# Attention chunks taken from four sequences in turn, scores masked by VectorE on their way out of PSUM, and first-expert weight loads tied to later blocks

## The chip, the core and the metric

The kernel runs on one core of a Trainium2 chip. The metric is the device time of one execution in microseconds (us). TensorE (PE) multiplies matrices, VectorE (DVE), ScalarE (ACT) and GpSimd (POOL) work on elements, and SyncE (SP) issues the transfers. Each engine takes its own instructions strictly in the order in which they stand.

## What is computed

Three layers stand one after another. The tokens are 4 sequences of 768; a head has 48 columns, there are 8 heads, and 384 columns in all.

```python
# layer 1: decayed linear attention, per sequence and head
for t in range(S):
    state = alpha[:, :, t, :, None] * state + np.einsum('bhd,bhe->bhde', k[:, :, t], v[:, :, t])
    y[:, :, t] = np.einsum('bhd,bhde->bhe', q[:, :, t], state)
# layer 2: SiLU feed-forward, 384 -> 2048 -> 384
h = x @ w_in
x = (h * (1.0 / (1.0 + np.exp(-h)))) @ w_out
# layer 3: one expert of eight for each token, 384 -> 1024 -> 384, times its gate
expert_idx = np.argmax(logits, axis=1)
out[mask] = gate_w[mask, None] * (np.maximum(x[mask] @ w1[e], 0.0) @ w2[e])
```

## The kernel before

**Tiles.** Attention works on chunks of 128 tokens. There are 24, six to a sequence (`CPB` = 6), and chunk n belongs to sequence n // 6. The feed-forward works on 8 blocks of 384 tokens, so that three chunks make a block; a block takes 16 steps f. Each step is `mm1` (9 products, then SiLU on ACT, a second ACT copy and a DVE subtraction that split the result into a high and a low fp16 half) and `mm2` (9 products). Every operand of a product is split into a high and a low half; three products stand for one in full precision. At the end of a block `route` picks the expert of each token and scatters the token's row into a list of that expert (the first DVE instruction of `route` is `lg`, L868, three to a block). The experts then run over 29 tiles of 128 rows.

**One attention chunk.** `att_A` makes running products of the decays (DVE scans). `att_Bk` and `att_Bq` scale keys and queries. `att_C` multiplies them into two score tiles in PSUM, which ACT copies out with a scale (L676) and GpSimd masks in place by `affine_select` (L677). `att_S` splits each masked tile: ACT copies the high half (L687), DVE subtracts to get the low half (L688). `att_KT` scales the keys on GpSimd (L696), splits them (L698, L699) and turns them by a transposing DMA. `att_D` adds score and state products into `yp` (L716 with the state, L723 with the scores); `att_move` sends the result by a transposing DMA into the block's input. `att_U` multiplies keys and values (`up`, L752), decays the state on GpSimd (L759), adds on DVE (L764, or L768 in the first chunk of a sequence) and splits the state for the next chunk (`st`: ACT L770, DVE L771). A chunk that is the first of its sequence has no state to read; one that is the last has no `att_KT` and no `att_U`. Two state tiles take turns.

**Weights.** `conv_w` turns the feed-forward weights from float64 words into fp16 halves; this runs in the first block. `load_w1` loads one 512 KB piece of an expert's first matrix into the staging tile `work` and splits it (L492 on ACT, L493 on DVE); 16 such pieces, rows 0 to 255 of eight experts, make `weights_a`, and later generators hold the rest. `pump_w` starts one piece.

**What sets the order.** `block` writes the steps out, with `pump_j` taking one attention step before and after each `mm1`, and `pump_w` one weight piece every fourth f from block 1 on. The framework's scheduler then puts the instructions of each engine in an order of its own, and issues early what nothing holds back. `after` adds a dependency only to hold an instruction back: here the first two pieces of `weights_a` wait for `gates[8]`, the `mm1` of step 8 in block 0; the other pieces wait only for their half of `work`.

Of the kernel before, what the change touches and what calls it, by code (L numbers as in the profile page):

```python
# [272 lines left out]
def attention_silu_moe_kernel(  # L273
# [78 lines left out]
    nc.gpsimd.iota(tok, pattern=[[128, NCH]], base=0, channel_multiplier=1)  # L352
# [19 lines left out]
    if True:  # L372
# [61 lines left out]
        state = [stat.tile([128, NPAIR, 2 * D], FP32, name=f"state{i}") for i in range(2)]  # L434
# [122 lines left out]
        def load_w1(c, e):  # L557
            st = work[:, F * (e % 2):F * (e % 2 + 1)]
            ins = nc.sync.dma_start(out=st, in_=w1[e, c * 128:(c + 1) * 128, :])
            if c == 0 and e < 2:  # L560
                after(ins, gates[KF // 2])
            split(st, SW1, w1s["h"][c][:, e, :], w1s["l"][c][:, e, :])
            if c == 0:
                nc.vector.tensor_reduce(
                    out=guard("w1", 2.0 ** -6), in_=st[:, 0:64], axis=AXX, op=ALU.max, apply_absolute_value=True
                )
# [19 lines left out]
        def att_load(n, names):  # L586
            if n >= NCH:
                return
            b, c = divmod(n, CPB)
            for nm in names:  # L590
                t = nat[nm][n % len(nat[nm])]
                nc.sync.dma_start(
                    out=t[:, :, 0:D], in_=att_src[nm][b, :, c * 128:(c + 1) * 128, :].rearrange("h p d -> p h d")
                )
                ch.setdefault(n, {})[nm] = t
# [57 lines left out]
        def att_Bq(n):  # L653
            d = ch[n]
            pq = transpose4(flat(d["q"]))
            Q = a2.tile([128, NPAIR, 128], FP32, tag="Q", name="Q", bufs=1)
            nc.vector.scalar_tensor_tensor(out=Q, in0=d["P"], scalar=PCLIP, in1=pq, op0=ALU.min, op1=ALU.mult)
            d["Q"] = Q
            if n % CPB:
                qs = d["qs"] = a2.tile([128, 2, NPAIR, 128], FP16, tag="qs", name="qs", bufs=1)  # L660
                nc.scalar.activation(out=qs[:, 0], in_=Q, func=ACTF.Copy)
                nc.gpsimd.tensor_sub(out=qs[:, 1], in0=Q, in1=qs[:, 0])

        def att_C(n):
# [9 lines left out]
            for i in range(2):  # L674
                s = a2.tile([128, NPAIR, 128], FP32, tag="S", name="S")
                nc.scalar.activation(out=s, in_=sc[i], func=ACTF.Copy, scale=SST)  # L676
                nc.gpsimd.affine_select(  # L677
                    out=s, in_=s, pattern=[[0, NPAIR], [1, 128]], compare_op=ALU.is_ge, fill=0.0, base=0,
                    channel_multiplier=-1,
                )  # L680
                d["S"].append(s)

        def att_S(n):
            d = ch[n]
            ss = d["ss"] = a2.tile([128, 2, 2, NPAIR, 128], FP16, tag="ss", name="ss", bufs=1)
            for i, s in enumerate(d.pop("S")):
                nc.scalar.activation(out=ss[:, i, 0], in_=s, func=ACTF.Copy)  # L687
                nc.vector.tensor_sub(out=ss[:, i, 1], in0=s, in1=ss[:, i, 0])  # L688

        def att_KT(n):  # L690
            d = ch[n]
            if n % CPB == CPB - 1:
                return
# [12 lines left out]
        def att_D(n, g):  # L706
            d = ch[n]
            c = n % CPB
# [34 lines left out]
        def att_U(n):  # L743
            d = ch.pop(n)
            c = n % CPB
# [10 lines left out]
            new, old = state[(c + 1) % 2], state[c % 2]  # L756
            if c:
                wide = d["pe"][:, 1].rearrange("r (p o) -> r p o", o=1).to_broadcast([128, NPAIR, 2 * D])
                nc.gpsimd.tensor_tensor(out=new, in0=old, in1=wide, op=ALU.mult)  # L759
# [9 lines left out]
            st = ch[n + 1]["st"] = a2.tile([128, 2, NPAIR, 2 * D], FP16, tag="st", name="st")  # L769
            nc.scalar.activation(out=st[:, 0], in_=new, func=ACTF.Copy)  # L770
            nc.vector.tensor_sub(out=st[:, 1], in0=new, in1=st[:, 0])  # L771
# [44 lines left out]
        def mm1(j, f):  # L816
# [9 lines left out]
            if j == 0:  # L826
                gates[f] = ins
            g, gh, gl = g_u[f % 3]
# [381 lines left out]
        def block(j):  # L1210
# [8 lines left out]
            for f in range(KF):  # L1219
# [10 lines left out]
                if j and (f % 4 == 1 or done[0] >= NCH):  # L1230
                    pump_w()
# [118 lines left out]
```

## Time and profile before

| | us |
|---|---|
| median of 3 runs | 847.2 (845.36 to 847.26) |
| profiled execution | 848.5 |
| its span | 846.9 |
| PE busy in the span | 758.5 |
| DVE busy | 517.5 |
| ACT busy | 441.0 |
| POOL busy | 256.6 |

Busy time is an average over stages which have different limits, so the span is read in stretches. On PE a row's duration includes the filling of the pipeline, so that a PE that shows as busy need not be at its peak. The chain of waits of the page covers only the last instructions and is of no use here.

### The profile page before, as it was taken

How to read it: one execution, taken by the hardware profiler on the slowest of the kernel's cores; microseconds unless marked ns; L12 is line 12 of the kernel's file. 1: busy time of each engine (PE TensorE's matmuls, PEld its weight loads, DVE VectorE, ACT ScalarE, POOL GpSimd, SP SyncE). 2: the span in 40 equal slices, each digit the busy share in tenths (PEclk: the TensorE clock that was granted, in tenths of full speed). 3: DMA queues.
4: the chain of work that ended last, by engine and by line, in shares of the span. 5: the costliest groups of instructions: out<-in, count | busy, mean ns of one | idle time of the engine just before them, and what ended most of it. 6: DMA issues, size and time to landing. Idle time of an engine off the chain costs nothing. (4 is left out here: it accounts for less than half of the span.)

```text
span 846.9 us, 16786 instructions
## 1 busy us (share of the span) xinstructions
PE 758.5 (90%) x5544; PEld 466.8 (55%) x5544; DVE 517.5 (61%) x1480; ACT 441.0 (52%) x953; POOL 256.6 (30%) x332
## 2 busy tenths in 40 slices
PE   5246899899999999999899999999688999999996
PEld 4144666556667666666657655555344554555553
DVE  8889899797787786766656486475552222222221
ACT  4456567776566565556555575666532222222221
POOL 4465221245453444234335112121331111111011
PEclk8556999999999999999999999999999999999999
DMA  9983754875445534413601146254767657655662
GB/s 203 266 237 60 162 135 129 202 182 112 94 77 107 89 70 87 80 46 72 82 27 36 32 150 178 75 141 147 173 160 143 127 112 105 110 119 106 115 122 63
DMA packets 250363, 100.23 MB, mean 118 GB/s; under 512 B 231305, under 2 KB 239662, under 8 KB 250144
## 3 DMA queue, kind: packets, MB, share of 16 engines
q1 hardware_dynamic: 246880, 89.50, 50.2%
q0 software_dynamic: 3392, 9.57, 3.3%
q8 instruction: 51, 0.84, 0.4%
q14 instruction: 40, 0.33, 0.1%
HBM read 58.40 MB, written 12.36 MB: 84 GB/s over the span
## 5 line engine op out<-in xcount | busy, mean ns | idle before, releaser
L843 PE MATMUL o<-wo_h,w2l 128*128 128x392 f16 x528 | 146.2, 330 | 9.1 <-ACT w2l L830 3.6
L822 PE MATMUL hp<-w2h,wi_h 128*128 128x384 f16 x576 | 145.9, 330 | 5.3 <-DMA w2h<-ys 3.0
L1140 DVE SCALAR_TENSOR_TENSOR work<-hp,work 128x512 f16<-128x512 f32 x58 | 40.0, 690 | 118.7 <-ACT work L1139 118.6
L1133 PE MATMUL hp<-w1h,xT 128*128 x348 | 106.1, 387 | 3.5 <-DVE work L1140 2.9
L843 PEld LDWEIGHTS <-w2l 128*128 128x128 f16 x792 | 73.8, 98 | 62.1 <-ACT w2l L830 5.8
L822 PEld LDWEIGHTS <-wi_h 128*128 128x128 f16 x768 | 74.1, 98 | 52.1 <-issue 8.2
L822 PE MATMUL hp<-w2h,wi_l 128*128 128x384 f16 x288 | 95.0, 330 | 1.3 <-DVE wi_l L493 1.3
L1133 PEld LDWEIGHTS <-xT 128*128 128x128 f16 x522 | 51.7, 99 | 64.6 <-issue 8.7
L843 PE MATMUL o<-wo_l,w2l 128*128 128x392 f16 x264 | 86.9, 329 | 0.0
L1168 POOL DMA_INDIRECT out_dram<-ob,mt x29 | 28.2, 972 | 188.5 <-ACT ob L1165 182.1
L1139 ACT ACTIVATE work<-hp 128x512 f16<-128x512 f32 x58 | 34.6, 596 | 72.5 <-PE hp L1133 68.7
L831 DVE SCALAR_TENSOR_TENSOR w2l<-w2l 128x384 f16<-128x384 f32 x88 | 51.8, 591 | 26.2 <-ACT w2l L830 26.2
L843 PE MATMUL o<-wo_h,g 128*128 128x392 f16 x240 | 67.0, 329 | 0.9 <-DVE wo_h L551 0.5
L1133 PE MATMUL hp<-w1l,xT 128*128 x174 | 67.0, 385 | 0.0
L829 ACT ACTIVATE w2l<-hp 128x384 f32<-128x384 f32 x88 | 42.6, 484 | 32.9 <-PE hp L822 25.9
L688 DVE TENSOR_TENSOR ss<-S,ss 128x512 f16<-128x512 f32 x48 | 38.9, 822 | 22.5 <-ACT ss L687 22.5
L822 PEld LDWEIGHTS <-wi_l 128*128 128x128 f16 x384 | 37.8, 98 | 25.4 <-DVE wi_l L493 1.7
L1157 PEld LDWEIGHTS <-work 128*128 128x128 f16 x336 | 33.4, 99 | 29.0 <-DMA work<-work 4.9
L1157 PE MATMUL po<-w2h,work 128*128 x224 | 44.8, 332 | 4.2 <-DMA work<-work 4.2
L822 PE MATMUL hp<-w2l,wi_h 128*128 128x384 f16 x192 | 47.5, 326 | 0.0
L830 ACT ACTIVATE w2l<-w2l 128x384 f16<-128x384 f32 x88 | 45.6, 520 | 2.6 <-PE o L843 1.1
L843 PEld LDWEIGHTS <-g 128*128 128x128 f16 x360 | 34.1, 98 | 22.5 <-issue 0.7
(258 smaller groups left out, 1612.0 us busy)
## 6 DMA issues: line engine op xcount, KB each, us to landing
work<-in_moe_w_dram SPq DMA_DIRECT2D x24, 512.0 KB, 4.1
work<-in_moe_w_dram SPq DMA_DIRECT2D x30, 384.0 KB, 3.2
nat_a<-in_alpha_dram SPq DMA_DIRECT2D x24, 192.0 KB, 3.5
nat_k<-in_k_dram SPq DMA_DIRECT2D x24, 192.0 KB, 3.6
nat_q<-in_q_dram SPq DMA_DIRECT2D x24, 192.0 KB, 3.1
nat_v<-in_v_dram SPq DMA_DIRECT2D x24, 192.0 KB, 2.8
w1h<-in_moe_w_in_dram SPq DMA_DIRECT2D x6, 768.0 KB, 5.6
w1h<-in_moe_w_out_dram SPq DMA_DIRECT2D x5, 768.0 KB, 8.1
```

Source lines behind the costliest of these rows:

```text
L688: nc.vector.tensor_sub(out=ss[:, i, 1], in0=s, in1=ss[:, i, 0])
L822: ins = nc.tensor.matmul(out=hp, lhsT=wi[a][f // 2][:, c, (f % 2) * 128:(f % 2 + 1) * 128], rhs=x[:, c, :], start=(n == 0), stop=(n == 3 * ...
L829: nc.scalar.activation(out=g, in_=hp, func=ACTF.Silu, scale=1.0 / (SX * SWI))
L830: nc.scalar.activation(out=gh, in_=g, func=ACTF.Copy, scale=SG)
L831: nc.vector.scalar_tensor_tensor(out=gl, in0=g, scalar=SG, in1=gh, op0=ALU.mult, op1=ALU.subtract)
L843: nc.tensor.matmul(out=acc[t], lhsT=a[:, ts], rhs=wo[w][f // 2][:, f % 2, :], start=(f == 0 and n == 0), stop=(f == KF - 1 and n == 2),)
L1133: nc.tensor.matmul(out=hp, lhsT=xT[:, a, :], rhs=w1s[w][c][:, bass.ds(d["e"], 1), fs], start=(n == 0), stop=(n == 3 * KD - 1),)
L1139: nc.scalar.activation(out=hs[:, 0], in_=hp, func=ACTF.Relu)
L1140: nc.vector.scalar_tensor_tensor(out=hs[:, 1], in0=hp, scalar=0.0, in1=hs[:, 0], op0=ALU.max, op1=ALU.subtract)
L1157: nc.tensor.matmul(out=po, lhsT=hT[c // 4][:, (a + c % 4) * 128:(a + c % 4 + 1) * 128], rhs=w2s[w][c][:, bass.ds(d["e"], 1), :], start=(n ...
L1168: nc.gpsimd.indirect_dma_start(out=out[:, :], out_offset=bass.IndirectOffsetOnAxis(ap=d["row"], axis=0), in_=ob, in_offset=None, bounds_ch ...
```

## The change

Four things are changed.

- Chunk n is now chunk n // 4 of sequence n % 4. The first four chunks have no state to read, the last four write none. There are four state tiles, each updated in place, and `tok` gives the token numbers in the new order. The split of the state (`st`) moves from the end of `att_U` to `att_Bq` of the chunk that reads it.
- The masked score tile is made by one DVE instruction that reads PSUM, multiplies by the scale and by a 0/1 tile `causal`; the ACT copy and the GpSimd `affine_select` go.
- The subtraction for the low half of the scores moves from DVE to GpSimd.
- Each of the 16 pieces of `weights_a` waits for the `mm1` written last before it, and `pump_w` starts in block 2 in place of block 1.

```diff
-    nc.gpsimd.iota(tok, pattern=[[128, NCH]], base=0, channel_multiplier=1)
+    nc.gpsimd.iota(tok.rearrange("p (c b) -> p c b", b=B), pattern=[[128, CPB], [S, B]], base=0, channel_multiplier=1)
...
-        state = [stat.tile([128, NPAIR, 2 * D], FP32, name=f"state{i}") for i in range(2)]
+        causal = stat.tile([128, 128], FP16, name="causal")
+        nc.vector.memset(causal, 1.0)
+        nc.gpsimd.affine_select(
+            out=causal, in_=causal, pattern=[[1, 128]], compare_op=ALU.is_ge, fill=0.0, base=0, channel_multiplier=-1
+        )
+        state = [stat.tile([128, NPAIR, 2 * D], FP32, name=f"state{i}") for i in range(B)]
...
-            if c == 0 and e < 2:
-                after(ins, gates[KF // 2])
+            if c < 2:
+                after(ins, gates["now"])
...
-            b, c = divmod(n, CPB)
+            c, b = divmod(n, B)
...
-            if n % CPB:
+            if n >= B:
...
+                st, cur = a2.tile([128, 2, NPAIR, 2 * D], FP16, tag="st", name="st"), state[n % B]
+                nc.scalar.activation(out=st[:, 0], in_=cur, func=ACTF.Copy)
+                nc.vector.tensor_sub(out=st[:, 1], in0=cur, in1=st[:, 0])
+                d["st"] = st
...
-                nc.scalar.activation(out=s, in_=sc[i], func=ACTF.Copy, scale=SST)
-                nc.gpsimd.affine_select(
-                    out=s, in_=s, pattern=[[0, NPAIR], [1, 128]], compare_op=ALU.is_ge, fill=0.0, base=0,
-                    channel_multiplier=-1,
+                nc.vector.scalar_tensor_tensor(
+                    out=s, in0=sc[i], scalar=SST, in1=causal.rearrange("p (o t) -> p o t", o=1).to_broadcast([128, NPAIR, 128]),
+                    op0=ALU.mult, op1=ALU.mult,
...
-                nc.vector.tensor_sub(out=ss[:, i, 1], in0=s, in1=ss[:, i, 0])
+                nc.gpsimd.tensor_sub(out=ss[:, i, 1], in0=s, in1=ss[:, i, 0])
...
-            if n % CPB == CPB - 1:
+            if n // B == CPB - 1:
...
-                nc.gpsimd.tensor_tensor(out=new, in0=old, in1=wide, op=ALU.mult)
+                nc.gpsimd.tensor_tensor(out=new, in0=new, in1=wide, op=ALU.mult)
...
-            st = ch[n + 1]["st"] = a2.tile([128, 2, NPAIR, 2 * D], FP16, tag="st", name="st")
-            nc.scalar.activation(out=st[:, 0], in_=new, func=ACTF.Copy)
-            nc.vector.tensor_sub(out=st[:, 1], in0=new, in1=st[:, 0])
...
+            gates["now"] = ins
...
-                if j and (f % 4 == 1 or done[0] >= NCH):
+                if j > 1 and (f % 4 == 1 or done[0] >= NCH):
```

The scheduler makes a new order on every engine. On SP's queue, in block 0, the rows of before stood so (`work` is the staging tile of the expert weights, `nat_*` are a chunk's inputs, `w2h` a block's input, `KT` the turned keys):

```order
L734 DMA_TRANSPOSE w2h_179<-ys 128x6x128
L559 DMA work<-in_moe_w_dram 128x1024 x2
L592 DMA nat_v_194<-in_v_dram 128x8x48
L559 DMA work<-in_moe_w_dram 128x1024
L592 DMA nat_a_190<-in_alpha_dram 128x8x48
L559 DMA work<-in_moe_w_dram 128x1024 x4
L592 DMA nat_k_186<-in_k_dram 128x8x48
L592 DMA nat_q_182<-in_q_dram 128x8x48
L559 DMA work<-in_moe_w_dram 128x1024 x2
```

Of the change, the first such loads on SP stand in block 2:

```order
L597 DMA nat_q_183<-in_q_dram 128x8x48
L564 DMA work<-in_moe_w_dram 128x1024
L742 DMA_TRANSPOSE w2h_177<-ys 128x6x128
L597 DMA nat_v_194<-in_v_dram 128x8x48
L597 DMA nat_a_190<-in_alpha_dram 128x8x48
L597 DMA nat_k_186<-in_k_dram 128x8x48
L597 DMA nat_q_182<-in_q_dram 128x8x48
L564 DMA work<-in_moe_w_dram 128x1024
L709 DMA_TRANSPOSE KT<-kd 128x8x128
```

The 16 loads, which stood together from the middle of block 0 to the middle of block 1, now stand singly, four to a block in blocks 2 to 5.

On GpSimd's queue, one chunk of the middle of the program before (`S` is a masked score tile, `K` and `kd` the keys, `qs` the queries' low half, `state` the decay of the state):

```order
L624 TENSOR_SCALAR pend<-P 128x4 x2
L696 TENSOR_TENSOR K<-K,pend 128x512
L677 AFFINE_SELECT S<-S 128x512 x2
L699 TENSOR_TENSOR kd<-K,kd 128x512
L662 TENSOR_TENSOR qs<-Q,qs 128x512
```

and of the change (`ss` is the low half of the scores):

```order
L629 TENSOR_SCALAR pend<-P 128x4 x2
L767 TENSOR_TENSOR state_200<-state_200,pend 128x384
L696 TENSOR_TENSOR ss<-S,ss 128x512
L704 TENSOR_TENSOR K<-K,pend 128x512
L696 TENSOR_TENSOR ss<-S,ss 128x512
L707 TENSOR_TENSOR kd<-K,kd 128x512
L667 TENSOR_TENSOR qs<-Q,qs 128x512
```

The key scaling, which went ahead of both score tiles, now stands between the two subtractions on which PE's score products wait.

## Rows read from the trace of the kernel before

**Rows 1.** The page: busy tenths and granted clock in 40 slices.

```profile
PE   5246899899999999999899999999688999999996
DVE  8889899797787786766656486475552222222221
PEclk8556999999999999999999999999999999999999
```

**Rows 2.** Windows: stretch, its length, busy us (x instructions) per engine, clock, DMA.

```profile
core 0: us, PE busy (x) PEld busy (x) DVE busy (x) ACT busy (x) POOL busy (x), PEclk, DMA share, GB/s
0.00:75.00 75.00, 32.67 (x297) 26.20 (x298) 65.48 (x141) 35.97 (x63) 39.08 (x53) 0.61 0.95 212
75.00:168.00 93.00, 82.64 (x745) 55.94 (x744) 84.95 (x195) 64.82 (x119) 25.16 (x27) 0.96 0.58 142
...
497.00:547.00 50.00, 47.60 (x290) 27.03 (x288) 31.29 (x109) 32.12 (x66) 11.25 (x13) 1.00 0.48 142
...
core 0: us, DVE busy (x), PEclk, DMA share, GB/s
...
6.00:168.00 162.00, 147.64 (x315) 0.80 0.75 176
```

**Rows 3.** First block: last move into it, first `mm1`, a stretch of SP's queue, `lg`.

```profile
71.56 1.22 SPq L734 DMA_TRANSPOSE w2h<-ys  x1
...
74.50 0.80 PE L822 MATMUL hp<-w2h,wi_h 128*128 128x384 f16 x2 [2.26 <-DMA w2h<-ys]
...
133.44 12.69 SPq L559 DMA_DIRECT2D work<-in_moe_w_dram  x4
146.18 0.91 SPq L592 DMA_DIRECT2D nat_k<-in_k_dram  x1
...
L868 DVE TENSOR_SCALAR lg<-o,itau x24: 126/218/227, 167.8 to 615.1; 128x8 f32<-128x8 f32 x24
```

**Rows 4.** Groups by line: operands, count, busy us, mean ns, idle before.

```profile
L688 DVE TENSOR_TENSOR ss<-S,ss 128x512 f16<-128x512 f32 x48 | 38.9, 822 | 22.5 <-ACT ss L687 22.5
...
L677 POOL TENSOR_SCALAR_AFFINE_SELECT S<-S 128x512 f32<-128x512 f32 x48 | 33.3, 706 | 37.7 <-ACT S L676 37.3
...
L687 ACT ACTIVATE ss<-S 128x512 f16<-128x512 f32 x48 | 29.4, 630 | 12.1 <-POOL S L677 12.1
L493 DVE SCALAR_TENSOR_TENSOR w1l<-work,w1h 128x1024 f16<-128x1024 f32 x24 | 29.2, 1218 | 9.5 <-ACT w1h L492 9.5
...
L676 ACT ACTIVATE S<-sc 128x512 f32<-128x512 f32 x48 | 26.7, 586 | 15.0 <-PE sc L671 12.8 <-DVE ss L688 2.2
L699 POOL TENSOR_TENSOR kd<-K,kd 128x512 f16<-128x512 f32 x20 | 25.8, 1289 | 3.2 <-ACT kd L698 2.9
...
L696 POOL TENSOR_TENSOR K<-K,pend 128x512 f32<-128x512 f32 x20 | 24.9, 1244 | 20.0 <-PE sc L671 19.8
...
L657 DVE SCALAR_TENSOR_TENSOR Q<-P,ptr 128x512 f32<-128x512 f32 x24 | 16.2, 673 | 0.3 <-PE ptr L603 0.2
```

**Rows 5.** Timeline: DVE instructions alone and beside GpSimd instructions with two inputs.

```profile
133.34 0.55 DVE L831 SCALAR_TENSOR_TENSOR w2l<-w2l 128x384 f16<-128x384 f32 x1
...
284.08 1.16 POOL L699 TENSOR_TENSOR kd<-K,kd 128x512 f16<-128x512 f32 x1 [0.17 <-ACT kd L698]
...
284.44 1.21 DVE L831 SCALAR_TENSOR_TENSOR w2l<-w2l 128x384 f16<-128x384 f32 x1 [3.06 <-ACT w2l L830]
...
289.18 1.16 POOL L662 TENSOR_TENSOR qs<-Q,qs 128x512 f16<-128x512 f32 x1 [3.94 <-ACT qs L661]
289.29 0.72 DVE L764 SCALAR_TENSOR_TENSOR state<-up,state 64x192 f32<-64x192 f32 x2 [0.77 <-PE up L752]
```

**Rows 6.** Timeline: the scores of one chunk in block 2, from PSUM to their low half.

```profile
282.04 1.06 ACT L676 ACTIVATE S<-sc 128x512 f32<-128x512 f32 x2
...
286.18 1.28 DVE L688 TENSOR_TENSOR ss<-S,ss 128x512 f16<-128x512 f32 x2
```

**Rows 7.** Waits of PE between 160 and 440 us: releaser, total, times, longest.

```profile
PE up L752 <- DMA KT<-kd: 4.0, 6, 2.5
...
PE yp L723 <- DVE ss L688: 1.1, 2, 0.6
```

More of the change, by code (lines that the diff above doesn't have):

```diff
@@ L707, in att_D @@
             d = ch[n]
-            c = n % CPB
+            c = n // B
             if g == 0:
@@ L744, in att_U @@
             d = ch.pop(n)
-            c = n % CPB
+            c, b = divmod(n, B)
             if c == CPB - 1:
@@ L755, in att_U @@
                     )
-            new, old = state[(c + 1) % 2], state[c % 2]
+            new = state[b]
             if c:
                 wide = d["pe"][:, 1].rearrange("r (p o) -> r p o", o=1).to_broadcast([128, NPAIR, 2 * D])
-                nc.gpsimd.tensor_tensor(out=new, in0=old, in1=wide, op=ALU.mult)
+                nc.gpsimd.tensor_tensor(out=new, in0=new, in1=wide, op=ALU.mult)
             for i in range(2):
```

## The prediction

> **What bounds the kernel now.** I read the slices first, then windows of the stretches, then the groups by line, and last single places of the timeline. The slices [rows 1] show two regimes. From the fifth slice on PE is at nine tenths nearly everywhere; in the first four it stands at 2 to 6 while DVE stands at 8 and 9, and the granted clock is at 5 to 8 tenths. So the start belongs to DVE. The windows put numbers to it [rows 2]: up to 75 us PE is busy for 32.67 us; DVE is busy for 147.64 of the 162 us between 6 and 168. The first `mm1` of block 0 starts at 74.50, right behind the landing of a move issued at 71.56, and the first `lg`, which closes block 0, comes at 167.8 [rows 3]. Block 0 thus takes 93 us, and in that stretch PE (82.64 us) and DVE (84.95 us) are both at nine tenths: neither has much to give there unless the other gives too. A block with almost no attention in it takes 50.00 us, of which PE is busy 47.60 [rows 2]. So what is late up to 168 us is first DVE, then DVE and PE together; behind that it is PE's own work plus short waits.
>
> The execution that is traced took 848.5 us, with a span of 846.9; the median of the runs is 847.2, which is 1.3 below it. The sum is made against 848.5 and 1.3 is taken off at the end.
>
> **The expert loads, at the start.** In before, 11 of the 16 DVE splits of `weights_a` stand ahead of the first `lg` in DVE's order; in the change none does. At 1218 ns each [rows 4] that is 13.4 us of DVE work that leaves the stretch in which DVE is busy 147.64 of 162 us. The loads also leave SP's queue, where four of them held it for 12.69 us, with the inputs of a later chunk behind them [rows 3].
>
> **The masked scores, at the start.** Ahead of the first `lg`, 13 subtractions at 822 ns (10.7 us) leave DVE and 14 masking instructions come. Before has no such instruction; the nearest row is the scale-and-multiply of the queries, which reads one PSUM and one SBUF operand of the same size, 673 ns [rows 4], so 9.4 us. Both bounds are close to that: 586 ns for the ACT copy out of PSUM, 822 for the old subtraction. Net 1.3 us out. The reordering of chunks takes one `st` split (under 1 us) and little else out of DVE before `lg`, and moves the state products of chunks 1 and 2 behind the start of block 0.
>
> On GpSimd, 14 subtractions at 1289 ns (the same shape in the keys' split) replace 13 masks at 706 [rows 4]: 18.0 against 9.2 us, 8.8 us more of an engine that is busy 39.08 of the first 75 us [rows 2]; its own time hides. What it does to DVE is another matter. A DVE split alone takes 0.55 us; one which met a two-input GpSimd instruction took 1.21, ending 0.41 us after that one; DVE instructions that read PSUM took their usual time beside another (0.72 for two) [rows 5]. The Trainium skill says it so: in "SBUF — State Buffer", section "Who interferes with whom", a DVE instruction with two SBUF inputs contends with a GpSimd instruction that reads SBUF, and the later one waits for the whole of the other. By that rule the trace agrees, and the rule speaks against moving the subtraction to GpSimd; if each of the 14 met one DVE instruction at full price the start would lose 9 us, and if none did it would lose nothing. From the rows: 14 times 0.66 us is 9.2 us, the lower end is 0, because the old subtraction with its mean of 822 ns paid for such meetings too and is gone. I take 1 us, near the lower end for that reason.
>
> Sum at the start: 13.4 + 1.3 − 1 = 13.7, say **14 us off**, if DVE's idle time there stays what it is (14.4 us). PE must find the same time: 10.4 us are free in its 93 us of block 0 and 42 in the first 75, so of the 14 at least 3.6 must come from an earlier first `mm1`, and at most all 14, which puts it at 60 to 71 us; fewer DVE instructions stand ahead of it, so that it can. The bounds: 4 us, if only the free time that the splits take from block 0's end comes back; 20, if the shorter state path and the free SP queue also take waits away.
>
> **Block 1.** The five other splits leave it too, 6 us of DVE and as much of ACT, beside PE that is busy there almost throughout. I take 1 us off (0 to 4).
>
> **The state path.** `up` now stands about 22 block products after `yp`, where it followed at once, and the transposed keys have that long to land. The waits of `up` for them between 160 and 440 us were 4.0 us in all [rows 7]: 3 off (0 to 4). The state itself is read four chunks later and is late nowhere.
>
> **The loads, where they go.** 16 splits return in blocks 2 to 5, four to a block, on ACT and DVE with time to spare, behind steps f that need these engines too. The nearest row is the block from 497 to 547: 14 splits stand in it and PE is idle for 2.40 of its 50.00 us [rows 2], 0.17 for each split. 16 of them cost 2.7, say **3 us** (0, where they fall into free time, to 1.2 each, 19, where each holds up one step fully). Each load now waits for an `mm1`, and behind it on SP stand the inputs of chunks two ahead, a move needed two blocks later and now and then the transposed keys; the last are needed at least one f later. I cost this wait at nothing; without that cover a wait of `up` of up to 2.5 us [rows 7] could return at each.
>
> **The scores' new path, blocks 1 to 5.** Of all terms this one is the least known. PE's order leaves 20 to 22 block products, four transposes and three state products between a chunk's scores and the first product that needs their halves; at 0.164 us each (47.60 us for 290 [rows 2]) and under 1 us for the rest that is 4.2 us. In before it was 23 to 29 with eight transposes, and the products that need the second low half stood farther on still. The path itself goes mask 673, ACT high half 630, GpSimd low half 1289, key scaling 1244, GpSimd low half 1289 [rows 4], 5.1 us; without the key scaling between, 3.9. So a chunk waits between 0 and 0.9 us, for 17 chunks (7 to 23) 0 to 15. I take 0.35, nearer to the lower end because the waits of PE for the low half were 1.1 us in all in before [rows 7], so the order had then been laid out to fit: **6 us on**. ACT is relieved of 48 copies of 586 ns, on no path that PE is seen to wait for.
>
> Total: −14 − 1 − 3 + 3 + 6 = −9; 848.5 − 9 = 839.5, less 1.3: **838 us**. The experts behind 601 us are untouched: from block 6 on every weight piece stands where it stood.
>
> **The rivals.** *The scores' path turns into a wait (slower).* In before the pure durations from the first copy to the second low half are 586 + 586 + 706 + 630 + 822 = 3.3 us, but the chunk of the timeline needed from 282.04 to 287.46 (286.18 being the start of the last two, 1.28 their time), 5.4 us [rows 6]: 2.1 us went into queues. If the new path keeps the key scaling inside (0.9 us too long) and one meeting of DVE and GpSimd per chunk (0.66), each chunk waits 1.56 us, 17 of them 26 us. Instead of 6 on that is 26: 848.5 − 15 + 26 = 859.5, less 1.3: 858. It decides from about 0.9 us a chunk. For it: GpSimd's subtraction is the last step and is 1.5 times as long as DVE's. Against it: PE waited for GpSimd nowhere in before. The rule of the Trainium skill cited above would act here, by 0.66 us a chunk. *The start is not DVE's (no change).* The first `mm1` comes earlier, but block 0 is then paced by the conversions of its own weights, and only the lower bound of 4 us comes back: 848.5 + 10 − 9 = 849.5, less 1.3 is 848 with the other terms as they are, and 842 if the scores' path costs nothing. I put it at 847. *The path fits (faster still).* No chunk waits and the state waits are all gone: −14 − 1 − 4 + 1 = −18, 829. That the loads are not moved at all is excluded by SP's order.
>
> **How the numbers follow.** The forecast, 831 to 844, has a chance of 0.50; the still faster case 0.20; no change 0.12; the slower case 0.18. About 0.3% (2.5 us) is what a measurement of this kernel can tell from no change. Faster is 0.50 + 0.20 = 0.70, the same 0.12, slower 0.18. The range runs from 822, which takes in most of the faster case, to 853, short of the middle of the slower one: about two in ten are outside.
>
> **What would show it.** In the profile of the changed kernel the first `mm1` should start at 60 to 71 us and the first `lg` come at 151 to 157; the DVE splits of `weights_a` should lie four to a block from block 2 on. `up` should wait for the transposed keys hardly at all. If PE waits in the table of waits for the low half of the scores (now released by GpSimd) exceed 10 us, the path was mis-sized; if `lg` comes after 162, the start was. The mask should take about 0.67 us and the GpSimd subtraction 1.15 to 1.3. The stretch from the last `lg` to the end should be as long as before.

## The result, and the profile of the changed kernel

The changed kernel takes 853.5 us (median; 852.8 to 854.5) beside 847.2 for the kernel before: a ratio of 1.0079, 95% interval 1.006 to 1.0097. It is slower by some 0.7%, where 838 was forecast and the range ended at 853. The profiled execution took 853.55, its span is 851.9 (848.5 and 846.9 before).

The page of the changed kernel, totals by engine and then busy tenths in 40 slices (compare [rows 1]):

```profile
PE 765.4 (90%) x5544; PEld 473.9 (56%) x5544; DVE 525.8 (62%) x1481; ACT 416.2 (49%) x905; POOL 278.7 (33%) x335
PE   5346899999999999999999999999797999999995
DVE  8989897877877897777767476466552222222221
```

PE executes as many instructions as before, 5544, but is busy for 765.4 us where it was 758.5. So 6.9 us more of PE's own time stand against a span that is 5.0 longer, and PE's idle time even went down by 1.9. The slices show the same two regimes as before.

The next view cuts both executions at two events, the first `lg` of block 0 and the first `lg` of block 5. Its columns are the stretch, its length, PE's busy time with the number of its instructions, and the granted clock. First the kernel before:

```profile
0.00:167.80 167.80, 115.11 (x1039) 0.81 0.75 173
167.80:496.60 328.80, 319.05 (x2723) 0.99 0.40 82
496.60:846.90 350.30, 324.39 (x1786) 0.98 0.57 126
```

Then the changed kernel:

```profile
0.00:161.80 161.80, 111.29 (x1011) 0.80 0.64 144
161.80:499.80 338.00, 329.86 (x2747) 0.99 0.46 98
499.80:851.90 352.10, 324.26 (x1788) 0.98 0.58 125
```

The first `lg` comes 6.0 us earlier, but in that stretch PE was also busy for 3.8 us less, partly because work is left for later (28 instructions): only 2.2 us are idle time that went. Blocks 1 to 5 are 9.2 us longer, with PE busy for 10.8 us more and idle for 1.6 less. The last stretch is 1.8 longer with the same work.

Which instructions got dearer shows where PE multiplies the scores. One chunk in block 1, timeline of PE (start, us, line, operands, count; matmuls overlap, so the step to the next start is what counts). The kernel before:

```profile
205.23 1.17 PE L671 MATMUL sc<-Q,K 64*128 64x128 f32 x16
206.33 0.34 PE L843 MATMUL o<-wo_h,w2l 128*128 128x392 f16 x1
```

The changed kernel:

```profile
221.33 1.16 PE L680 MATMUL sc<-Q,K 64*128 64x128 f32 x8
222.42 0.51 PE L849 MATMUL o<-wo_h,g 128*128 128x392 f16 x2
...
224.84 1.16 PE L680 MATMUL sc<-Q,K 64*128 64x128 f32 x8
225.93 0.34 PE L827 MATMUL hp<-w2l,wi_h 128*128 128x384 f16 x1
```

In before, the 16 records of a chunk took 1.10 us from their start to the next instruction's. In the change the first eight alone take 1.09 us, and the other eight 1.09 more behind a dozen block products. A score product uses 64 of PE's 128 rows. In before, products of head half 0 (rows 0 to 63) and half 1 (rows 64 to 127) stood in turn, and two such neighbours started 13 ns apart; in the change four of one half stand together, then four of the other, and each record starts 0.11 us or more behind the last.

By "pair" I mean below a score record that starts under 30 ns ahead of PE's next, and by "score time" the sum of the steps from each score record to PE's next start, a longer gap counted as 0.25 us; both are worked out from the 384 score records. Before had 105 pairs (13 chunks of 24 at eight each, and one more) and 39.3 us; the change has 53 and 47.5. Cut at the first `lg` of block 0, the loss stands out more: in blocks 1 to 5 the pairs fell from 80 to 8 and the score time rose from 26.2 to 35.9 us, which is 9.7 of the 10.8 us found above, while ahead of that `lg` the pairs rose from 25 to 45 and the score time fell by 1.4. The Trainium skill states a ground for it in "TensorEngine Tiling (Array Packing)", section "Key Properties": tiles of the array work independently and can run in parallel. The trace agrees, with 16 records in 1.10 us next to each other and 8 in 1.09 us apart.

Waits of PE in the whole changed kernel (waiting tile, releaser, total, times, longest; compare [rows 7]):

```profile
PE sc L680 <- DVE Q L662: 7.6, 2, 7.3
...
PE yp L731 <- POOL ss L696: 4.0, 4, 1.5
```

The wait for GpSimd's low halves, on which the slower rival rested, is 4.0 us, all of it in the first 75 us.

### The profile page after: what moved, and what is told of

Its sections match the earlier page's. It is cut to its first block, busy times and chain, and to the rows that moved or that the text cites. A ratio compares the mean times of both kernels' runs of the same rounds, so it can differ in the third digit from the quotient of the medians.

```text
span 851.9 us, 16790 instructions
## 1 busy us (share of the span) xinstructions
PE 765.4 (90%) x5544; PEld 473.9 (56%) x5544; DVE 525.8 (62%) x1481; ACT 416.2 (49%) x905; POOL 278.7 (33%) x335
## 5 line engine op out<-in xcount | busy, mean ns | idle before, releaser
L827 PEld LDWEIGHTS <-wi_h 128*128 128x128 f16 x768 | 74.7, 99 | 56.7 <-issue 11.5
L849 PE MATMUL o<-wo_l,w2l 128*128 128x392 f16 x264 | 87.7, 332 | 0.0
L837 DVE SCALAR_TENSOR_TENSOR w2l<-w2l 128x384 f16<-128x384 f32 x88 | 60.2, 687 | 31.4 <-ACT w2l L836 30.4
L696 POOL TENSOR_TENSOR ss<-S,ss 128x512 f16<-128x512 f32 x48 | 59.8, 1250 | 27.0 <-ACT ss L695 26.1
L680 PE MATMUL sc<-Q,K 64*128 64x128 f32 x384 | 51.1, 308 | 11.1 <-DVE Q L662 7.6
L680 PEld LDWEIGHTS sc<-Q,K 64*128 64x128 f32 x384 | 42.9, 208 | 21.6 <-DVE Q L662 8.1
L835 ACT ACTIVATE w2l<-hp 128x384 f32<-128x384 f32 x88 | 41.8, 480 | 23.0 <-PE hp L827 16.4
```

The costliest lines, as they stand in the source:

```text
L680: nc.tensor.matmul(out=sc[i][:, p, :], lhsT=d["K"][r, p, :], rhs=d["Q"][r, p, :], start=True, stop=True)
L696: nc.gpsimd.tensor_sub(out=ss[:, i, 1], in0=s, in1=ss[:, i, 0])
L827: ins = nc.tensor.matmul(out=hp, lhsT=wi[a][f // 2][:, c, (f % 2) * 128:(f % 2 + 1) * 128], rhs=x[:, c, :], start=(n == 0), stop=(n == 3 * ...
L835: nc.scalar.activation(out=g, in_=hp, func=ACTF.Silu, scale=1.0 / (SX * SWI))
L837: nc.vector.scalar_tensor_tensor(out=gl, in0=g, scalar=SG, in1=gh, op0=ALU.mult, op1=ALU.subtract)
L849: nc.tensor.matmul(out=acc[t], lhsT=a[:, ts], rhs=wo[w][f // 2][:, f % 2, :], start=(f == 0 and n == 0), stop=(f == KF - 1 and n == 2),)
```

## The experiments

The table gives for each kernel the ratio of its time to that of the kernel before on the same chip, and from its profiled execution the pairs, the score time, PE's idle time (span less busy) and the first `lg`. Executions of one kernel lie mostly within 5 us on either side of their median (the farthest, one of after_one, 8), so that a profiled execution can stand off its ratio; verdicts go by the ratios.

| kernel | ratio (95%) | pairs | score us | idle us | first lg |
|---|---|---|---|---|---|
| before | 1 | 105 | 39.3 | 88.4 | 167.8 |
| the change | 1.0079 (1.006 to 1.0097) | 53 | 47.5 | 86.4 | 161.8 |
| after_again (the change once more) | 1.0060 (1.0037 to 1.0084) | 53 | 47.8 | 85.0 | 162.4 |
| after_paired | 1.0044 (1.0024 to 1.0065) | 93 | 42.1 | 86.9 | 161.7 |
| after_chain | 1.0048 (1.0027 to 1.0070) | 158 | 35.8 | 94.0 | 161.1 |
| before_halves | 1.0098 (1.0079 to 1.0116) | 36 | 48.7 | 84.3 | 168.8 |
| before_chain | 0.9965 (0.9949 to 0.9981) | 149 | 35.9 | 87.7 | 172.3 |
| before_loads | 0.9993 (0.9970 to 1.0016) | 102 | 39.5 | 89.0 | 156.7 |
| before_loads_chain | 0.9981 (0.9963 to 1.0000) | 157 | 34.2 | 91.0 | 159.9 |
| before_turns | 1.0112 (1.0087 to 1.0137) | 44 | 48.0 | 82.7 | 167.1 |
| before_turns_chain | 0.9923 (0.9896 to 0.9949) | 149 | 36.5 | 80.7 | 168.8 |
| turns_chain_again | 0.9932 (0.9910 to 0.9954) | 149 | 36.5 | 83.3 | 169.0 |
| before_mask | 1.0103 (1.0075 to 1.0132) | 56 | 46.8 | 89.9 | 173.1 |
| before_mask_chain | 1.0068 (1.0046 to 1.0089) | 160 | 35.0 | 92.3 | 178.2 |
| mask_chain_one | 0.9932 (0.9906 to 0.9959) | 154 | 36.2 | 83.9 | 171.4 |
| mask_chain_ssdve | 1.0188 (1.0151 to 1.0225) | 160 | 35.0 | 104.4 | 181.0 |
| after_nomask_chain | 0.9960 (0.9941 to 0.9978) | 149 | 36.4 | 86.1 | 157.6 |
| after_one | 1.0013 (0.9989 to 1.0037) | 48 | 48.5 | 76.8 | 159.3 |
| after_chain_one | 0.9951 (0.9933 to 0.9970) | 156 | 36.5 | 81.2 | 156.6 |

**Do the pairs matter?** The theory was that lost pairs are the loss (A), the rival that they don't matter (B). after_chain keeps the two halves side by side in PE's order (`behind` is a dependency that orders and waits for nothing); before_chain is the same edit in the kernel before:

```diff
-            for p in range(NPAIR):
-                for i in range(2):
+            prev = None
+            for p in range(NPAIR):
+                for i in (1, 0):
...
+                    if prev is not None:
+                        behind(ins, prev)
+                    prev = ins
```

> The changed kernel, with one thing added: in PE's order the score products of the two heads of a pair stand side by side (head 1 of a pair first, then head 0, and so on in turn), by an order-only dependency from each to the next. 151 neighbours of different halves stand in PE's order, 45 in the changed kernel and 80 in the kernel before. Nothing else is edited. Theory A (pairs): two score products that use different halves of the 128 rows and stand next to each other start 13 ns apart and take 0.11 us together; apart they take 0.11 us each. The changed kernel has 53 such pairs in the trace against 105, and in blocks 1 to 5, where PE never waits, this is time. It expects some 150 pairs, score time of PE from 47.5 down to 33 to 38 us, and a time of 839 to 847, below the changed kernel's 853.5 and not above the kernel before. Theory B (the pairs do not matter; the time went to the state products of 33 chunks that moved out of the start, and to the longer DVE and GpSimd instructions): 852 to 855, as the changed kernel.

> The kernel before, with the order-only dependencies of the first run of this set: 150 neighbours of different halves instead of 80. Theory A: 140 to 160 pairs instead of 105, 40 to 50 times 0.11 to 0.16 us is 4 to 8 us, of which a part lies in the start: 840 to 845. Theory B: 846 to 849.

after_paired lets the two PSUM banks come free together; a tile of scores takes its bank in turn from three, and by the order in which tiles are taken that of half 1 is the one which the state update of the chunk before leaves:

```diff
+                    if p == 0 and i == 0 and turn[0] is None and n - 1 in freed:
+                        after(ins, freed[n - 1])
...
-                    nc.vector.scalar_tensor_tensor(
+                    freed[n] = nc.vector.scalar_tensor_tensor(
                         out=dst, in0=src, scalar=SST / (SK * SV), in1=dst, op0=ALU.mult, op1=ALU.add
                     )
```

> The changed kernel, with one thing added: from block 0 on, the first score product of a chunk waits for the last update of the state by the chunk before, which is what frees the PSUM bank of the second half of the scores. The two halves then find their banks free together; 80 neighbours of different halves stand in PE's order, as many as in the kernel before (45 in the changed kernel). Theory A: about 100 pairs in the trace, score time near 40 us, and a time 4 to 8 us below the changed kernel: 845 to 849. Theory B: no change, 852 to 855.

before_halves takes the pairs from the kernel before:

```diff
-            for p in range(NPAIR):
-                for i in range(2):
-                    r = slice(64 * i, 64 * i + 64)
+            for i in range(2):
+                r = slice(64 * i, 64 * i + 64)
+                for p in range(NPAIR):
```

> The kernel before, with one thing changed: the loop over the two halves of the scores is the outer one and that over the pairs of heads the inner one, so that PE's order has four products of one half and then four of the other. 14 neighbours of different halves are left of 80. Theory A: 20 pairs or fewer instead of 105, 85 times 0.11 to 0.16 us is 9 to 14 us of PE's time, of which some 3 lie in the start, where PE waits anyway: 853 to 858. Theory B: 846 to 849, as the kernel before.

The score chunk of block 1 in before_halves, timeline of PE:

```profile
206.11 1.71 PE L671 MATMUL sc<-Q,K 64*128 64x128 f32 x16
```

Theory B falls: in the kernel before, taking pairs away costs 1.0% (score time up by 9.4 us, PE busy 766.7) and adding them gains 0.35% (score time down by 3.4). One wait on the state update brought the pairs of the change from 53 to 93. But theory A was too simple for the change itself. There the chain took 11.7 us off the score time and only 0.1 to 0.3% off the total; after_chain and after_paired, at 851.7 and 851.1 us, miss what theory A expected of them and stay above before. In after_chain PE waited instead, in the whole kernel (0.6 and 4.0 us in the change):

```profile
PE up L770 <- DMA KT<-kd: 7.0, 6, 4.2
PE yp L741 <- POOL ss L706: 6.7, 10, 1.5
```

The dependency moved more of PE's order than the scores. Of the 14 chunks whose `up` lies between 160 and 500 us, the change has 13 in which `up` stands 21 to 26 block products behind the chunk's last `yp`; in after_chain `up` follows at once in all of them. PE's idle time in blocks 1 to 5 rose from 8.1 to 16.4 us, and the two waits above are 5.3 us between 160 and 500 us. That is a part of the lost gain; the rest is open here, also because the profiled execution of after_chain lies 3.9 us above its median.

**One part at a time.** before_loads has the later loads alone, before_loads_chain with the chain on top:

```diff
-            if c == 0 and e < 2:
-                after(ins, gates[KF // 2])
+            if c < 2:
+                after(ins, gates["now"])
...
-                if j and (f % 4 == 1 or done[0] >= NCH):
+                if j > 1 and (f % 4 == 1 or done[0] >= NCH):
```

> The kernel before with only the third part of the change: the loads of the first expert weights wait for the latest block product of their moment, and start with block 2 instead of block 1. PE's order keeps 79 neighbours of different score halves (80 before, 45 in the change). If the start is DVE's and its 11 w1 splits are what the change gains there, the first product of block 0 starts at 66 to 71 us instead of 74.5, the first lg comes at 160 to 164 instead of 167.8, the 16 splits hide in blocks 2 to 5, and the time is 840 to 845. If the start gain of the change came from its other parts, the first lg stays at 166 to 169 and the time at 846 to 850.

> The kernel before with the later loads and with the order-only dependencies that keep score products of different halves side by side (154 neighbours). If the two gains add, about 3 us of pairs and what the loads bring alone, 4 to 6 us: 838 to 842. If PE can use only one of them, 843 to 846.

before_turns has the chunks in turn alone (`b, c = divmod(n, CPB)` becomes `c, b = divmod(n, B)`, four states, `st` made in `att_Bq`):

> The kernel before with only the first part of the change: chunks of the four sequences in turn, four states, state halves made with the queries. 43 neighbours of different score halves are left of 80. Theory A (lost pairs are the loss): score time of PE from 39 up to 46 to 49 us, some 7 us more in blocks 1 to 5 where PE hardly waits; the start gives back 0 to 3: 850 to 855. Rival (the pairs went with the scores' new path alone): 845 to 849.

before_mask has the scores' path alone:

```diff
-                nc.scalar.activation(out=s, in_=sc[i], func=ACTF.Copy, scale=SST)
-                nc.gpsimd.affine_select(
+                nc.vector.scalar_tensor_tensor(
...
-                nc.vector.tensor_sub(out=ss[:, i, 1], in0=s, in1=ss[:, i, 0])
+                nc.gpsimd.tensor_sub(out=ss[:, i, 1], in0=s, in1=ss[:, i, 0])
```

> The kernel before with only the second part of the change: DVE masks and scales the scores on their way out of PSUM, GpSimd makes the low halves. 45 neighbours of different score halves are left of 80. Theory A: score time of PE up to 46 to 49 us, the time 850 to 855, with PE waiting for GpSimd's low halves less than 3 us behind the start. Rival (the scores' path becomes a wait, the slower case of the prediction): PE waits 10 us or more for GpSimd's low halves in blocks 1 to 5, the time 857 or more. Rival (the pairs went with the turns alone): 845 to 849.

The loads were forecast to carry the gain and bring none that can be told from nothing; before_loads_chain, at 847.0 us, lies above both of its forecasts. Windows of PE in before_loads, cut at the same two events:

```profile
0.00:156.70 156.70, 108.01 (x1006) 0.80 0.67 147
156.70:495.70 339.00, 324.74 (x2761) 1.00 0.46 98
```

The first `lg` comes 11.1 us earlier, which is what the lost splits should do. The first `mm1` does not move, though 66 to 71 us were expected: it starts at 74.50 in before and here at

```profile
74.51 0.80 PE L822 MATMUL hp<-w2h,wi_h 128*128 128x384 f16 x2 [2.16 <-DMA w2h<-ys]
```

The splits all stand behind it in before (duration in ns, least, median and most, then first and last start in us):

```profile
L493 DVE SCALAR_TENSOR_TENSOR w1l<-work,w1h x24: 1196/1222/1231, 128.7 to 509.1; 128x1024 f16<-128x1024 f32 x24
```

But the gain is mostly work put off: PE was busy for 7.1 us less ahead of that `lg`. PE's busy time of block 0 fell from 82.9 to 75.6 us and that of block 1 rose from 62.2 to 68.7. Only 4.0 us of idle time went, and in blocks 1 to 5 PE's idle time grew by 4.5 (339.00 less 324.74, against 9.75). Between 160 and 500 us there `up` waits for the transposed keys for 8.3 us (4.0 in before between 160 and 440, [rows 7]), as the prediction had warned:

```profile
PE up L752 <- DMA KT<-kd: 8.3, 10, 1.8
```

before_turns and before_mask each lose the pairs on their own and are slower by 1.0 to 1.1%. That cost is not paid twice in the change, where both come together.

**The same parts, pairs kept.** before_mask_chain and before_turns_chain add the chain to the two kernels above.

> The kernel before with the scores' new path alone (mask and scale on DVE out of PSUM, low halves on GpSimd), and with the order-only dependencies that keep score products of different halves side by side (152 neighbours; 45 without them, 80 before). Theory A (the path alone lost 8.3 us because of the pairs): the score time of PE falls from 46.8 to 34 to 38 us and the time to 844 to 848, beside 844.7 for the kernel before with the same dependencies. Rival (the path costs by itself, by longer DVE and GpSimd instructions or by waits for the low halves): 850 or more, with PE's idle time up by 4 us or more.

> The kernel before with the chunks in turn alone, and with the same order-only dependencies (150 neighbours; 43 without). Theory A: score time of PE from 48.0 to 34 to 38 us, the time from 857.9 to 843 to 849. Rival (taking chunks in turn costs by itself): 852 or more.

> The changed kernel once more, beside the two others on one chip, so that runs with the dependencies can be set against it. By its first measure the ratio to the kernel before is 1.006 to 1.010, the score time of PE 47 to 48 us and PE's idle time 86 us; the runs with the dependencies in the changed kernel were at 1.0048.

With pairs, chunks in turn are a gain: at 0.9923 their loss is gone with the missing pairs. The scores' path is not: at 1.0068 it stands 1.0% (8.7 us) above before_chain, theory A fails here, and its rival holds.

**What the scores' path costs.** The first `lg` of before_mask comes at 173.1, 5.3 us later than before, and DVE is busier ahead of it by 8.8 us. Windows of DVE from 6 us to the first `lg`, before, before_mask and the change:

```profile
6.00:167.80 161.80, 147.44 (x314) 0.80 0.75 176
```

```profile
6.00:173.10 167.10, 156.22 (x317) 0.98 0.75 175
```

```profile
6.00:161.80 155.80, 137.18 (x285) 0.79 0.64 145
```

14 masks of 675 ns put in 9.2 us up to there (by 168 us in before, 13 subtractions had 10.9), so that about 10.5 us came on top: 1.2 for one weight split more ahead of that `lg` (12 against 11), and some 9 for other DVE instructions that got longer. In before_mask (timeline), DVE and then GpSimd, one instruction and two:

```profile
59.77 1.51 DVE L484 TENSOR_SCALAR w1l<-w1h 128x768 int32<-128x768 int32 x1
```

```profile
57.16 3.70 POOL L692 TENSOR_TENSOR ss<-S,ss 128x512 f16<-128x512 f32 x2
```

In before the same shift of a weight piece had no GpSimd instruction beside it:

```profile
57.69 0.55 DVE L479 TENSOR_SCALAR w1l<-w1h 128x768 int32<-128x768 int32 x1
```

Theory C: GpSimd's two-input subtractions stretch DVE at the start. mask_chain_one gives GpSimd one input, mask_chain_ssdve takes the work off it:

```diff
-                nc.gpsimd.tensor_sub(out=ss[:, i, 1], in0=s, in1=ss[:, i, 0])
+                nc.gpsimd.tensor_scalar(out=ss[:, i, 1], in0=s, scalar1=0.0, scalar2=None, op0=ALU.mult)
```

> The kernel before with the scores' new path and the order-only dependencies, and with one instruction changed: where GpSimd subtracts the high half from the masked scores (two inputs), it multiplies the masked scores by zero (one input), so that the low halves of the scores are zero, which leaves their part out of the computation. DVE keeps the mask. Theory C (the path's own cost is at the start, where GpSimd's two-input subtractions stretch DVE's weight conversions: a shift of 0.55 us alone took 0.9 to 2.0 beside them): DVE's busy time up to the first lg falls from 154 to 147 to 150 us, the first lg comes at 170 to 174 instead of 178.2, the time falls by 4 to 8 us to 847 to 851 or a ratio of 0.998 to 1.002. Rival (DVE pays for the mask itself, or PE for the longer path): the first lg stays at 176 to 179, the ratio at 1.005 to 1.009.

> The kernel before with the mask on DVE out of PSUM but the low halves left on DVE too, and with the order-only dependencies. GpSimd has no work on the scores any more. Some 14 subtractions at 0.55 to 0.85 us (8 to 12 us) come back to DVE ahead of the first lg, and the meetings with GpSimd go. Theory C: the two are about equal, the first lg at 175 to 180 and the ratio 1.004 to 1.009. If the meetings cost little, the first lg comes at 182 or later and the ratio is above 1.01; if they cost more than the subtractions, the first lg is at 174 or earlier.

The groups of before_mask_chain, DVE's low half of the SiLU tiles and GpSimd's subtraction (busy us, mean ns, idle before):

```profile
L845 DVE SCALAR_TENSOR_TENSOR w2l<-w2l 128x384 f16<-128x384 f32 x88 | 56.6, 644 | 39.5 <-ACT w2l L844 38.2 <-PE o L857 1.2
...
L702 POOL TENSOR_TENSOR ss<-S,ss 128x512 f16<-128x512 f32 x48 | 62.4, 1308 | 40.8 <-ACT ss L701 40.7
```

The same of mask_chain_one:

```profile
L845 DVE SCALAR_TENSOR_TENSOR w2l<-w2l 128x384 f16<-128x384 f32 x88 | 51.9, 594 | 28.8 <-ACT w2l L844 28.8
...
L702 POOL TENSOR_SCALAR ss<-S 128x512 f16<-128x512 f32 x48 | 74.1, 1559 | 22.1 <-DVE S L691 21.7 <-POOL K L710 0.2
```

GpSimd's instruction became longer, 1559 against 1308 ns, and yet the ratio fell from 1.0068 to 0.9932 and the first `lg` from 178.2 to 171.4: this speaks for theory C, and against a rival that rests on how long GpSimd takes. DVE's busy time from 6 us to the first `lg`, before_mask_chain and mask_chain_one:

```profile
6.00:178.20 172.20, 153.88 (x319) 0.76 0.73 172
```

```profile
6.00:171.40 165.40, 149.92 (x318) 0.96 0.76 181
```

It fell by 4.0 us, as theory C expected, and in the change the same edit (after_one below) takes it from 137.2 to 132.9. Of the SiLU low halves, 21 that met GpSimd's subtraction in before_mask_chain took 0.91 us on average; 21 that met the one-input instruction took 0.57, and those that met no subtraction or the like on GpSimd 0.55 and 0.56.

Three things more differ. The one-input form does not wait for ACT's high half, so that GpSimd starts earlier; PE multiplies by low halves that are zero; and the scheduler's order is another, with `up` 10 to 30 block products behind `yp` where it followed at once in before_mask_chain. In before_mask_chain PE waited for a high or low half for 2.4 us (1.7 in mask_chain_one), and `up` waited for 1.5 us in blocks 1 to 5, so that the first and the third can be worth little there. The zeros were not tested alone. The gain, 1.4%, is more than I forecast, and more than the start: of the 13.4 us between the two spans 6.8 lie ahead of the first `lg`, and a part of these may be the clock, granted at 0.76 there in the profiled execution of before_mask_chain and at 0.96 in that of mask_chain_one; 4.1 lie in blocks 1 to 5, and 2.5 behind them, where no scores are made. So some 4 us of DVE's time at the start are shown as the price of the meetings; that they are the whole of the 1.4% is not.

With the subtractions on DVE it is slower still, 1.0188, where theory C expected 1.004 to 1.009, and more than 1.01 was to mean that the meetings cost little. This run cannot price them. The first `lg` comes at 181.0, only 2.8 us later than in before_mask_chain. Blocks 1 to 5 are 14.1 us longer, with PE idle for 16.2 us against 3.6, and `up` waits for the transposed keys, between 181 and 512.3 us, for 12.8 us (0.5 in blocks 1 to 5 of before_mask_chain):

```profile
PE up L766 <- DMA KT<-kd: 12.8, 9, 2.3
```

Why the keys come late there is open.

**Do the two causes make up the loss?** after_nomask_chain is the change with the old scores' path and the chain; turns_chain_again repeats the best version beside it. after_one and after_chain_one are the change with the one-input instruction, without and with the chain.

> The changed kernel with two things undone: the scores' path is that of the kernel before (ACT copy, GpSimd mask, DVE low halves), and score products of different halves stand side by side by order-only dependencies. Chunks in turn and later loads stay. If the lost pairs and the scores' path are the whole loss, this is the kernel with chunks in turn and pairs (ratio 0.9923) with the later loads on top (0 to 3 us): ratio 0.989 to 0.995, 839 to 844. If the later loads cost something once the chunks come in turn, 0.997 or more.

> The kernel before with the chunks in turn and the order-only dependencies, once more, beside the run with the later loads on one chip: ratio 0.990 to 0.995 as at first. A ratio of 0.997 or more would say that the first measure was of a few lucky runs.

> The changed kernel with one instruction changed: GpSimd multiplies the masked scores by zero (one input) where it subtracts (two inputs); the low halves of the scores are zero, which leaves their part out of the computation. The score products stay unpaired (42 neighbours of different halves; 45 in the changed kernel). If the meetings of GpSimd and DVE cost the changed kernel what they cost the kernel before with the same path, 0.9 to 1.4%: the ratio falls from 1.006 to 1.008 to 0.994 to 1.000. If in the changed kernel, with 11 w1 splits fewer at the start, the meetings fall into free time: 1.003 to 1.008.

> The same, and score products of different halves side by side by order-only dependencies (150 neighbours). With both causes out, the ratio should be that of chunks in turn with pairs, 0.988 to 0.995; if a third cause is left in the changed kernel, 0.998 or more.

Within what the runs can tell, they do. In the change itself, with the one-input instruction the ratio is 1.0013, between the two cases that I forecast, and with the pairs kept too 0.9951, which is 1.1 to 1.3% below the change (1.0060 and 1.0079) in two steps of about 0.6%. The chain brought half of that or less while the meetings were there. after_nomask_chain, at 0.9960, just misses the 0.995 that I expected: beside 0.9932 the later loads may cost 0.3%, and in before_loads_chain against before_chain 0.2%, but the intervals of both comparisons overlap. A gain by the loads shows nowhere.

Chunks in turn with the chain, and nothing else of the change, was the fastest complete version: 0.9923 and 0.9932, some 6 us below the kernel before and 12 below the change.

## Why the prediction was wrong, point by point

**What bounds the kernel.** That the start is DVE's held: across the kernels the first `lg` follows DVE's busy time ahead of it (147.4 us and 167.8; 133.5 and 156.7; 156.2 and 173.1), though less closely with the chain (153.9 and 178.2 in before_mask_chain). That behind it the time is "PE's own work plus short waits" held too. The failing step comes after: PE's work was taken as given, and no term was made for its order. "PE's order" was read for distances between scores and their use, not for which score products stand next to each other. That term is 9.7 us more in blocks 1 to 5 of the change's trace, where nothing hides it, and 8.2 in the whole kernel.

Between the two profiled executions the start brought 6.0 us where 14 were forecast, blocks 1 to 5 lost 9.2 where 5 were forecast (−1 − 3 + 3 + 6), and 1.8 more were lost behind them. As the lost pairs alone make 9.7, the forecast terms of these blocks came to about nothing together; that the blocks were only 4 us off is luck.

**The start, 14 us off.** Mis-sized. The sum took 13.7 us of DVE's work out and held DVE's idle time at 14.4 us. Measured, DVE's busy time ahead of the first `lg` fell by 10.3 (147.4 to 137.2) and its idle time rose to 18.6, so that the first `lg` came at 161.8, 6.0 earlier and behind the 151 to 157 of the forecast. The subtractions' meetings were given 1 us of 0 to 9.2, "near the lower end"; they cost 4.3 us of DVE's time in the change, by after_one, and about 9 in before_mask. The reason given, that the old subtraction had paid for such meetings too, did not hold: other DVE instructions beside GpSimd's get longer, the shifts among them. The rule of the Trainium skill cited there ("SBUF — State Buffer", section "Who interferes with whom") also names `tensor_scalar` among those that can contend, which I had not weighed; the trace agrees, with 0.55 us alone and 1.51 beside. A further step was to count an earlier `lg` as an earlier end: PE was busy for 3.8 us less ahead of it, and 2.2 us were gained.

The first `mm1`, at 66.98, lies inside the forecast, but not by the lost splits: they stand behind it, and in before_loads it stayed at 74.51. It moved with the chunks in turn; before_turns, which keeps the splits, has it at

```profile
63.34 0.80 PE L823 MATMUL hp<-w2h,wi_h 128*128 128x384 f16 x2
```

**Block 1 and the state path.** Block 1 became 1.6 us shorter (1 forecast). `up` no longer waits for the transposed keys between 160 and 440 us, where it was 4.0 [rows 7]; in the whole kernel one wait of 0.6 us is left. 3 off was about right.

**The loads' return.** 3 us forecast, 4.5 us of idle time in before_loads, where `up`'s wait returned as feared; in the change that wait did not return, with `up` farther back, as forecast. In after_nomask_chain, which has the loads and the chunks in turn, `up` follows `yp` at once in most chunks, and there it waits for the keys for 8.2 us between 160 and 500.

**The scores' path, 6 us on.** Wrong in place. PE waits for the low halves nowhere behind 75 us in the change. With pairs kept the path costs 8.7 us by the ratios, of which some 4 are shown as DVE's longer instructions at the start. The mask took 673 ns and the subtraction 1250, both as forecast (groups of the changed kernel, GpSimd and DVE):

```profile
L696 POOL TENSOR_TENSOR ss<-S,ss 128x512 f16<-128x512 f32 x48 | 59.8, 1250 | 27.0 <-ACT ss L695 26.1
```

```profile
L685 DVE SCALAR_TENSOR_TENSOR S<-sc,causal 128x512 f32<-128x512 f32 x48 | 32.0, 673 | 0.3 <-PE sc L680 0.3
```

**The rivals.** The slower one had the right sign and named the meetings of DVE and GpSimd, but as a wait of PE for each chunk; it gave 858. The rival in which the start does not pay came near in effect, for other reasons. None spoke of the pairs.

**Open.** Why before_mask alone loses the pairs, with the chunks in their old order, was not followed up. The chain gained 0.35% on the scores' path but 1.9% on chunks in turn, with about the same score time taken off (11.8 and 11.5 us); that PE then waits for other things was seen in after_chain only. Every edit also moved other products in PE's order, `up` above all, and no run held the whole order fixed. Whether zeros in the low halves alone would change the time was not tested.

## What to carry to other kernels

Where an engine is full, an order that a scheduler makes is a cost of its own: look at what stands next to what, and hold neighbours together that share the array, by an order-only dependency, and look afterwards what else it moved. A marker that comes earlier is a gain only as far as the busiest engine did the same work ahead of it, so compare busy and idle time between markers, not the markers. An instruction moved to GpSimd is to be priced by what DVE does beside it, above all where DVE is late; here the number of its inputs mattered more than its length.

## What the runs showed of the hardware that was not expected

Two fp32 score products on different halves of the rows start 13 ns apart when they are neighbours in PE's order, and a chunk of 16 records takes 1.10 us; with the halves apart it takes 2.18. A GpSimd instruction with one input, 1559 ns long, left a two-input DVE instruction beside it at 0.57 us on average, where one with two inputs, 1308 ns long, stretched it to 0.91. There the Trainium skill ("SBUF — State Buffer", section "Who interferes with whom") would have any GpSimd instruction that reads SBUF contend with a DVE instruction of two SBUF inputs; the measurement differs from it for this one-input form, though not all of the effect is gone everywhere: 0.67 us in after_one and 0.72 in after_chain_one, against 1.04 in the change and 1.05 in after_chain. The example is in mask_chain_one, DVE and then GpSimd:

```profile
269.26 0.56 DVE L845 SCALAR_TENSOR_TENSOR w2l<-w2l 128x384 f16<-128x384 f32 x1 [0.57 <-ACT w2l L844]
```

```profile
268.25 2.97 POOL L702 TENSOR_SCALAR ss<-S 128x512 f16<-128x512 f32 x2 [2.85 <-DVE S L691]
```
